# Retention in groups of 128 tokens, one of them shared by two batches, and one transfer queue issued in step with the outputs

## The chip, the cores and the metric

The kernel runs on one core of one Trainium2 chip. The core has a matrix engine (PE, with its weight loads PEld), a vector engine (DVE), an activation engine (ACT), a general engine (POOL) and a sequencer that only starts transfers (SP). Transfers can be started from SP (called SPq in the trace), ACT (ACTq) and POOL (POOLq). The metric is the device time of one execution in microseconds (us), the median of several runs.

## The reference

```
scores = (1/sqrt(64)) * q @ k^T             # 8 batches, 8 heads, 576 tokens, 64 wide
ret    = scores * gamma_h^(i-j)  for i >= j, else 0
x      = ret @ v                            # heads side by side: 4608 tokens x 512
h      = x @ w_in                           # 512 -> 2048
out    = (h * cos(h)) @ w_out               # 2048 -> 512, float32
```

## The kernel before

Retention is computed in chunks: each batch of 576 tokens is cut into four chunks of 128 and one of 64, so there are 40 chunks. `load` brings q, k and v of a chunk (float32, in pieces of 64 numbers) by three transfers from SP. `prep` scales q and k by powers of gamma (POOL, for the first four chunks k on DVE), casts v, and from chunk 8 on starts two DMA transposes on SP that turn scaled q and k into `qkT`; the first eight chunks are transposed on PE (`tr`). On PE a chunk is then: `scores` (tile `sc`, masked on DVE into `ret`), `state` (tile `st`, the running sum of k^T v of the batch, masked into `sb`), and `attn_out` (tile `ov`, from `sb` and from `ret`, copied on DVE into `xT`).

The two dense products run over ten tiles of tokens, `widths` = 512, 256, 256, then seven of 512; they are called tile 0 to 9 here. For a tile, `mm1` makes 16 blocks `h` (four matmuls each), ACT takes the cosine, DVE multiplies into `gT`; `mm2` then adds up 16 matmuls for each 128 tokens into `o`, ACT copies `o` to `ot`, and a transfer writes it out (output 0 to 35, one for each 128 tokens). The retention pieces of the next tile are laid between the `mm2` matmuls, after each four of them.

The order on each engine is the order of the code. `feed`, called from `scores`, issues loads and preps ahead: chunk c+4 is prepared and chunk c+10 loaded when chunk c has its scores. Outputs are started from ACT, loads and transposes from SP, weights from POOL (`w_in` in four parts, `w_out` in four parts). Three early loads wait for weight parts (`GATED`). Each transfer from SP or ACT takes the next of eight completion counters in the order in which the code issues it, and waits for the transfer that held this counter before it, whichever of the two queues that one stands in. PSUM has four buffers for `h` and `o`; `ot` has four buffers.

Of the kernel before, what the change touches and what calls it, by code (L numbers as in the profile page):

```python
# [17 lines left out]
def kernel(  # L18
# [13 lines left out]

    nc = tc.nc
# [8 lines left out]
    NC = (S + P - 1) // P  # L42
    csz = [min(P, S - c * P) for c in range(NC)]
# [8 lines left out]
    chunks = [(b, c) for b in range(B) for c in range(NC)]  # L52
# [22 lines left out]
    pos_i = consts.tile([P, NC, H], I32)  # L75
    pos = consts.tile([P, NC, H], F32)
    lng = consts.tile([P, H], F32)
    gq = consts.tile([P, NC, H], F32)
    gk = consts.tile([P, NC, H], F32)
    ln_scale = consts.tile([P, 1], F32)  # L80
    half_pi = consts.tile([P, 1], F32)
    tri = consts.tile([P, P], F32)
    diag2 = consts.tile([P, P], F32)
# [7 lines left out]
    def load(g):  # L91

        b, c = chunks[g]
        sz = csz[c]
        first = None
        for name, src in (("q", q), ("k", k), ("v", v)):
            f = ld.tile([P, H, D], F32, tag="f" + name, name=f"f{name}")
            i = nc.sync.dma_start(  # L98
                f[:sz], src[b, :, c * P : c * P + sz, :].rearrange("h s d -> s h d")
            )  # L100
            first = first or i
            tiles["f" + name, g] = f
        return first

    def prep(g, eng_k, eng_v):

        b, c = chunks[g]
        sz = csz[c]
# [3 lines left out]
        tq = gq[:sz, c, :].unsqueeze(2).to_broadcast([sz, H, D])  # L112
        tk = gk[:sz, c, :].unsqueeze(2).to_broadcast([sz, H, D])
        nc.gpsimd.tensor_tensor(out=qks[:sz, 0], in0=fq[:sz], in1=tq, op=ALU.mult)  # L114
        eng_k.tensor_tensor(out=qks[:sz, 1], in0=fk[:sz], in1=tk, op=ALU.mult)  # L115
        if eng_v is nc.scalar:
            nc.scalar.copy(vb[:sz], fv[:sz])
        else:
            eng_v.tensor_copy(vb[:sz], fv[:sz])  # L119
        qkT = trp.tile([P, 2, HG, P], BF16, tag="qkT", name="qkT")  # L120
        if g >= N_PE_T:
            for m in range(2):
                nc.sync.dma_start(  # L123
                    qkT[:, m, :, :sz],
                    qks[:sz, m].rearrange("s h d -> s (h d)"),
                    transpose=True,
                )
        tiles["a", g] = (qks, vb, qkT)

    def transposes(g):  # L130
        sz = csz[chunks[g][1]]
        qks, vb, qkT = tiles["a", g]
        ps = ps_ov.tile([P, 2, HG, P], BF16, tag="ov", name="tr")
        for m in range(2):
            for hg in range(HG):
                nc.tensor.transpose(  # L136
                    ps[:, m, hg, :sz],
                    qks[:sz, m, 2 * hg : 2 * hg + 2, :].rearrange("s h d -> s (h d)"),
                    ident[:sz, :sz],
                )  # L140
        nc.vector.tensor_copy(qkT[:, :, :, :sz], ps[:, :, :, :sz])  # L141

    def scores(g):
        if g >= 4:
            feed(g + 1 + LEAD)
        sz = csz[chunks[g][1]]
        qks, vb, qkT = tiles["a", g]
        ps = ps_sc.tile([P, 2, HG, P], F32, tag="sc", name="sc")
        for hg in range(HG):
            for he in range(2):  # L150
                d0 = he * D
                nc.tensor.matmul(  # L152
                    ps[:sz, he, hg, :sz],
                    lhsT=qkT[d0 : d0 + D, 1, hg, :sz],
                    rhs=qkT[d0 : d0 + D, 0, hg, :sz],
# [3 lines left out]
        ret = retp.tile([P, 2, HG, P], BF16, tag="ret", name="ret")  # L159
        nc.vector.tensor_tensor(  # L160
            out=ret[:sz, :, :, :sz].rearrange("p a b i -> p (a b) i"),
# [160 lines left out]
    for u in units(0, 4):  # L322
        u()
# [82 lines left out]
```

## Time and profile before

| | |
|---|---|
| median of 3 runs | 357.11 us (355.91 to 357.18) |
| the profiled execution | 357.89 us, of it 356.2 us span from the first to the last instruction |
| PE busy | 307.8 us (86%) |
| DVE, ACT, POOL busy | 200.1, 128.1, 105.6 us |
| read from HBM, written | 36.70 MB, 9.44 MB |

The span is what the trace shows; 1.7 us of the profiled time lie around it. An engine's share of busy time is a mean over stages that have different limits.

### The profile page before, as it was taken

The page shows a single profiled execution, that of the slowest core. Times are in us where ns is not written, and L with a number is a line of the kernel's source. Part 1 is how long each engine was busy: PE and PEld are TensorE (multiplying, and loading weights), DVE is VectorE, ACT ScalarE, POOL GpSimd, SP SyncE. Part 2 cuts the span into 40 slices and gives each one's busy share as a digit, 9 for nine tenths or more (in the row PEclk, how much of TensorE's full clock was granted, in tenths as well). Part 3 has the DMA queues.
Part 4 walks back from the last instruction along what each step waited for, and adds up shares of the span by engine and source line. Part 5 has one row for each costly group of instructions (what it writes and reads, how often), then busy time and mean ns, then how long its engine had stood idle before and what let it go on. Part 6 is the DMA issues. An engine that isn't in the chain of part 4 may idle for free.

```text
span 356.2 us, 5733 instructions
## 1 busy us (share of the span) xinstructions
PE 307.8 (86%) x2176; PEld 155.3 (44%) x2176; DVE 200.1 (56%) x299; ACT 128.1 (36%) x204; POOL 105.6 (30%) x128
## 2 busy tenths in 40 slices
PE   1078999203999999999999999999999999999995
PEld 0054445101747544454444444444444544454442
DVE  2387745000767858666853776486468648844710
ACT  2123700002708057107513831471175118414721
POOL 3630467705041640571055017502800300000000
PEclk9989999855799999999999999999999999999999
DMA  9999999999967997899679809961610310011011
GB/s 175 211 209 205 192 202 192 208 196 216 228 133 170 222 198 151 187 211 220 123 153 240 154 18 215 217 112 45 142 39 0 83 57 26 1 61 59 2 46 72
DMA packets 153180, 49.80 MB, mean 140 GB/s; under 512 B 144448, under 2 KB 148032, under 8 KB 153152
## 3 DMA queue, kind: packets, MB, share of 16 engines
q1 hardware_dynamic: 143744, 35.80, 56.3%
q10 hardware_dynamic: 5184, 9.44, 7.9%
q0 software_dynamic: 4224, 4.19, 7.1%
q8 instruction: 17, 0.28, 0.3%
q14 instruction: 11, 0.09, 0.1%
HBM read 36.70 MB, written 9.44 MB: 130 GB/s over the span
## 4 chain that ended last, share of the span: by engine, by line
PE 80%; DMA 7%; SPq 5%; DVE 4%; issue 1%; ACT 1%; POOL 1%; ACTq 0%; POOLq 0%
PE o L262 35%; PE h L246 35%; SPq L98 4%; PE ov L211 3%; PE sc L152 3%; DMA fk<-in_k_dram 3%; DMA qkT<-qks 2%; PE ov L201 2%; PE st L175 2%; DMA fv<-in_v_dram 2%; SPq L123 1%; DVE ret L160 1%; PE tr L136 1%; DVE qkT L141 1%; DVE xT L220 1%
## 5 line engine op out<-in xcount | busy, mean ns | idle before, releaser
L246 PE MATMUL h<-xT,w_in_sb 128*128 128x512 bf16 (+1 forms) x640 | 129.7, 364 | 23.4 <-ACT ot L271 21.8
L255 DVE TENSOR_TENSOR gT<-h,cosh 128x512 bf16<-128x512 f32 (+1 forms) x160 | 101.5, 638 | 76.7 <-ACT cosh L254 76.3
L262 PE MATMUL o<-w_out_sb,gT 128*128 128x512 bf16 x576 | 143.0, 380 | 0.7 <-DVE gT L255 0.7
L254 ACT ACTIVATE cosh<-h,half_pi 128x512 f32<-128x512 f32 (+1 forms) x160 | 101.5, 644 | 35.6 <-PE h L246 34.5
L246 PEld LDWEIGHTS <-w_in_sb 128*128 128x128 bf16 x640 | 63.8, 100 | 88.0 <-issue 24.8
L271 ACT COPY ot<-o 128x512 f32<-128x512 f32 x36 | 21.1, 585 | 172.9 <-PE o L262 150.3
L262 PEld LDWEIGHTS <-gT 128*128 128x128 bf16 x576 | 49.5, 98 | 50.7 <-issue 0.5
L119 POOL CAST vb<-fv 128x512 bf16<-128x512 f32 (+1 forms) x36 | 21.9, 608 | 132.4 <-PE ov L211 119.2
L114 POOL TENSOR_TENSOR qks<-fq,gq 128x512 bf16<-128x512 f32 (+1 forms) x40 | 41.6, 1040 | 42.1 <-DMA fq<-in_q_dram 30.0
L160 DVE TENSOR_TENSOR ret<-sc,tri 128x1024 bf16<-128x1024 f32 (+1 forms) x40 | 44.5, 1113 | 16.4 <-PE sc L152 16.4
L115 POOL TENSOR_TENSOR qks<-fk,gk 128x512 bf16<-128x512 f32 (+1 forms) x36 | 37.4, 1040 | 1.3 <-DMA fk<-in_k_dram 1.2
L220 DVE CAST xT<-ov 128x512 bf16<-128x512 f32 (+1 forms) x40 | 25.5, 637 | 17.5 <-PE ov L211 16.5
L184 DVE TENSOR_TENSOR sb<-st,diag_104 128x512 bf16<-128x512 f32 x32 | 22.0, 686 | 12.3 <-PE st L175 12.3
L136 PE MATMUL tr<-ident,qks 128*128 128x128 bf16 (+1 forms) x64 | 6.1, 249 | 17.2 <-DVE qkT L141 10.7
L152 PE MATMUL sc<-qkT 64*128 64x128 bf16 (+1 forms) x320 | 15.8, 221 | 1.6 <-DVE qkT L141 0.8
L211 PE MATMUL ov<-ret,vb 128*64 128x128 bf16 (+1 forms) x320 | 16.2, 224 | 0.6 <-DVE qkT L141 0.6
L152 PEld LDWEIGHTS <-qkT 64*128 64x128 bf16 (+1 forms) x320 | 9.3, 99 | 16.5 <-issue 14.5
L136 PEld LDWEIGHTS <-qks 128*128 128x128 bf16 (+1 forms) x64 | 4.8, 112 | 19.5 <-issue 9.5
L201 PEld LDWEIGHTS <-sb 128*128 128x128 bf16 x128 | 9.5, 100 | 8.3 <-issue 1.3
L211 PEld LDWEIGHTS <-vb 128*64 128x64 bf16 (+1 forms) x320 | 10.1, 111 | 6.5 <-issue 3.7
L175 PE MATMUL st<-vb,qks 128*128 128x128 bf16 x128 | 12.9, 225 | 0.0
L201 PE MATMUL ov<-qkT,sb 128*128 128x128 bf16 (+1 forms) x128 | 11.9, 218 | 1.0 <-DVE xT L220 0.6
(26 smaller groups left out, 32.0 us busy)
## 6 DMA issues: line engine op xcount, KB each, us to landing
out_dram<-ot ACTq DMA_DIRECT2D x36, 256.0 KB, 3.2
fq<-in_q_dram SPq DMA_DIRECT2D x32, 256.0 KB, 4.2
fk<-in_k_dram SPq DMA_DIRECT2D x32, 256.0 KB, 4.8
fv<-in_v_dram SPq DMA_DIRECT2D x32, 256.0 KB, 5.0
w_out_sb<-in_moe_w_out_dram POOLq DMA_DIRECT2D x4, 512.0 KB, 16.1
w_in_sb<-in_moe_w_in_dram POOLq DMA_DIRECT2D x1, 1024.0 KB, 11.4
fq<-in_q_dram SPq DMA_DIRECT2D x8, 128.0 KB, 3.6
fk<-in_k_dram SPq DMA_DIRECT2D x8, 128.0 KB, 3.9
```

What stands on the lines that cost most here:

```text
L114: nc.gpsimd.tensor_tensor(out=qks[:sz, 0], in0=fq[:sz], in1=tq, op=ALU.mult)
L115: eng_k.tensor_tensor(out=qks[:sz, 1], in0=fk[:sz], in1=tk, op=ALU.mult)
L152: nc.tensor.matmul(ps[:sz, he, hg, :sz], lhsT=qkT[d0 : d0 + D, 1, hg, :sz], rhs=qkT[d0 : d0 + D, 0, hg, :sz], start=True, stop=True,)
L160: nc.vector.tensor_tensor(out=ret[:sz, :, :, :sz].rearrange("p a b i -> p (a b) i"), in0=ps[:sz, :, :, :sz].rearrange("p a b i -> p (a b) i"),
L184: nc.vector.tensor_tensor(out=sb, in0=ps, in1=diag2.unsqueeze(1).to_broadcast([P, HG, P]), op=ALU.mult,)
L201: nc.tensor.matmul(ps[:, hg, :sz], lhsT=sb[:, hg, :], rhs=qkT[:, 0, hg, :sz], start=(hg == 0), stop=False, skip_group_check=True,)
L211: nc.tensor.matmul(ps[he * D : he * D + D, hg, :sz], lhsT=vb[:sz, 2 * hg + he, :], rhs=ret[:sz, he, hg, :sz], start=(c == 0 and hg == 0), ...
L220: nc.vector.tensor_copy(xT[:, :, t0 : t0 + sz], ps[:, :, :sz])
L246: nc.tensor.matmul(ps[:, :w], lhsT=w_in_sb[:, dg, et * P : (et + 1) * P], rhs=xT[:, dg, t0 : t0 + w], start=(dg == 0), stop=(dg == DG - 1),)
L254: nc.scalar.activation(cosh[:, :w], ps[:, :w], ACTF.Sin, bias=half_pi, scale=1.0)
L255: nc.vector.tensor_mul(gT[:, et, :w], ps[:, :w], cosh[:, :w])
L262: nc.tensor.matmul(ps, lhsT=gT[:, et, tsi * P : (tsi + 1) * P], rhs=w_out_sb[:, et, :], start=(et == 0), stop=(et == ET - 1),)
```

## The change

Chunks become 36 groups of 128 consecutive tokens. Two batches are nine groups (`PER`); the middle one (`MIX` = 4) holds the last 64 tokens of one batch and the first 64 of the next, is loaded by six transfers of half the size, has a mask of its own (`tri_mix`), and starts a new state from its second half. All transfers from SP stand in one order written in `feed(s)`, which is called once for each output s, just after its transfer, which moves from ACT to SP: up to 11 groups ahead are loaded, up to 9 prepared, and groups up to s+7 are transposed, by one DMA transpose of twice the width in the place of two. The first four groups are now prepared, transposed, scored and summed one after the other, where before all four were prepared first; the copies of `tr` into `qkT` move from DVE to ACT. The first tile's `mm1` runs over two halves of 256 tokens in an order of blocks written by hand (`first`), and in 256-wide tiles two blocks share a PSUM bank, one cosine and one product. In tile 0 the `mm2` matmuls run output by output, and retention of the next tile is put into their second half (`late`). Groups 4 and 5 wait for the second part of `w_out`.

```
-    AHEAD = 6
-    LEAD = 4
-    GATED = {4: 4, 5: 6, 6: 7}
+    NG = NTOK // P
+    PER = 2 * S // P
+    MIX = PER // 2
+    HP = P // 2
     N_PE_T = 8
...
-    ld = ctx.enter_context(tc.tile_pool(name="ld", bufs=7))
-    nat = ctx.enter_context(tc.tile_pool(name="nat", bufs=7))
-    trp = ctx.enter_context(tc.tile_pool(name="trp", bufs=7))
+    ld = ctx.enter_context(tc.tile_pool(name="ld", bufs=6))
+    nat = ctx.enter_context(tc.tile_pool(name="nat", bufs=8))
+    trp = ctx.enter_context(tc.tile_pool(name="trp", bufs=8))
...
+        if g % PER == MIX:
+            parts = [(0, HP, t0), (HP, P, t0 + HP)]
...
     def transposes(g):
         qks, vb, qkT = tiles["a", g]
         if g >= N_PE_T:
+            nc.sync.dma_start(qkT, qks.rearrange("s m h d -> s (m h d)"), transpose=True)
+            return
...
-        nc.vector.tensor_copy(qkT[:, :, :, :sz], ps[:, :, :, :sz])
+        nc.scalar.copy(qkT, ps)
     def scores(g):
-        if g >= 4:
-            feed(g + 1 + LEAD)
...
     def mm2(n, tsi, et):
...
             nc.scalar.copy(ot, ps)
-            t0 = starts[n] + tsi * P
-            nc.scalar.dma_start(out[t0 : t0 + P, :], ot)
+            s = starts[n] // P + tsi
+            nc.sync.dma_start(out[s * P : (s + 1) * P, :], ot)
+            feed(s)
+    def feed(s):
+        nonlocal loaded, prepared, transposed
+        while loaded < min(NG, 2 * s + 8, s + 11):
+            load(loaded)
+            loaded += 1
+        while prepared < min(NG, loaded, 2 * s + 7, s + 9):
+            prep(prepared)
+            prepared += 1
+            if transposed < N_PE_T:
+                transposed += 1
+        while transposed < min(prepared, s + 8):
+            transposes(transposed)
+            transposed += 1
...
     for g in range(4):
-        prep(g, nc.vector, nc.scalar)
-        if g == 2:
+        if g == 0:
+            prep(g, early=True)
+        if g == 3:
             load_w_in(0, 256)
             load_w_in(256, 512)
+            load_w_in(512, 1024)
+            load_w_in(1024, 2048)
+            w_dma = [load_w_out(e, e + 4) for e in range(0, ET, 4)]
+            load(4, gate=w_dma[1])
+            load(5)
...
+        transposes(g)
+        nc.scalar.copy(tiles["a", g][1], tiles.pop(("fv", g)))
+        scores(g)
+        state(g)
+        if g < 3:
+            prep(g + 1, early=True)
+            attn_out(g)
+    for g in (4, 5):
+        prep(g)
+    first = [(0, 0), (0, 4), (1, 0), (0, 8), (1, 4), (0, 12), (1, 8), (1, 12)]
+    for i, (half, et) in enumerate(first):
+        mm1(0, et, half * 256, 256)
+        if i == 0:
+            attn_out(3)
+        mm1(0, et + 2, half * 256, 256)
     for n, w in enumerate(widths):
...
-        if n == 0:
-            mms = [(tsi, et) for et in range(ET) for tsi in range(nts)]
-        else:
-            mms = [(tsi, et) for tsi in range(nts) for et in range(ET)]
+        mms = [(tsi, et) for tsi in range(nts) for et in range(ET)]
...
-            want = -(-total * (i + 1) // max(1, len(groups) - 2))
+            late = len(groups) // 2 if n == 0 else 0
+            want = -(-total * (i + 1 - late) // max(1, len(groups) - 2 - late))
             while todo and total - len(todo) < want:
                 todo.pop(0)()
```

First place, SP's queue when the first outputs are made. Before, from the last load of chunk 13 over the load of chunk 14 to the first DMA transposes (chunks 8 and 9); no output stands in this queue.

```order
L98 DMA fv_423<-in_v_dram 128x8x64
L98 DMA fq_596<-in_q_dram 64x8x64
L98 DMA fk_598<-in_k_dram 64x8x64
L98 DMA fv_600<-in_v_dram 64x8x64
L123 DMA_TRANSPOSE qkT_607<-qks_602 128x4x128 x2
L98 DMA fq_643<-in_q_dram 128x8x64
L98 DMA fk_645<-in_k_dram 128x8x64
L98 DMA fv_647<-in_v_dram 128x8x64
L123 DMA_TRANSPOSE qkT_654<-qks_649 128x4x64 x2
```

Now, from output 1 (ot_627) over the loads of groups 8 and 9 to the transpose of group 8 and output 2 (ot_710).

```order
L283 DMA out_0_dram<-ot_627 128x512
L102 DMA fq_630<-in_q_dram 128x8x64
L102 DMA fk_632<-in_k_dram 128x8x64
L102 DMA fv_634<-in_v_dram 128x8x64
L102 DMA fq_636<-in_q_dram 128x8x64
L102 DMA fk_638<-in_k_dram 128x8x64
L102 DMA fv_640<-in_v_dram 128x8x64
L137 DMA_TRANSPOSE qkT_650<-qks_648 128x8x128
L283 DMA out_0_dram<-ot_710 128x512
```

The outputs have moved into this queue, and a load stands behind the output that calls for it; before, all 15 first loads stood ahead of the first transpose. From here the queue goes on as output 2, loads 10 and 11, transpose 9, output 3, loads 12 and 13, transpose 10, output 4, load 14, transpose 11.

Second place, SP's queue now in the first of the 512-wide tiles behind the small ones (tile 3, outputs 8 to 11): the transpose of group 14, output 8 (ot_1522), the load of group 18, the transpose of group 15 (qkT_1343), output 9 (ot_1587).

```order
L137 DMA_TRANSPOSE qkT_1259<-qks_1257 128x8x128
L283 DMA out_0_dram<-ot_1522 128x512
L102 DMA fq_1525<-in_q_dram 128x8x64
L102 DMA fk_1527<-in_k_dram 128x8x64
L102 DMA fv_1529<-in_v_dram 128x8x64
L137 DMA_TRANSPOSE qkT_1343<-qks_1341 128x8x128
L283 DMA out_0_dram<-ot_1587 128x512
```

The transpose of group s+7 now stands behind output s and behind the load of group s+10; this pattern repeats for each output up to 25. Before, transposes and loads alternated in the same way, with the output in another queue.

Third place, ACT while tile 0 ends. Before, with the outputs' transfers between the copies:

```order
L254 ACTIVATE cosh<-h,half_pi 128x512 x16
L271 COPY ot<-o 128x512
L273 DMA out_dram<-ot 128x512
L271 COPY ot<-o 128x512
L273 DMA out_dram<-ot 128x512
```

Now:

```order
L264 ACTIVATE cosh<-h,half_pi 128x512 x16
L281 COPY ot<-o 128x512 x2
L147 COPY qkT<-tr 128x1024 x2
L281 COPY ot<-o 128x512 x2
L264 ACTIVATE cosh<-h,half_pi 128x512 x8
```

No transfer stands in ACT's order any more; two copies of transposed groups stand between the outputs' copies.

## Rows read from the trace of the kernel before

**Rows 1.** The page: forty equal slices of the span (8.9 us each).

```profile
PEclk9989999855799999999999999999999999999999
GB/s 175 211 209 205 192 202 192 208 196 216 228 133 170 222 198 151 187 211 220 123 153 240 154 18 215 217 112 45 142 39 0 83 57 26 1 61 59 2 46 72
```

**Rows 2.** PE by time: start, length, line, tile, idle before and what ended it.

```profile
63.91 0.60 PE L246 MATMUL h<-xT,w_in_sb 128*128 128x256 bf16 x4
82.73 1.01 PE L246 MATMUL h<-xT,w_in_sb 128*128 128x256 bf16 x4 [18.22 <-ACT ot L271]
...
96.53 1.03 PE L262 MATMUL o<-w_out_sb,gT 128*128 128x512 bf16 x4
...
107.40 1.91 PE L246 MATMUL h<-xT,w_in_sb 128*128 128x256 bf16 x16
109.64 5.40 PE L246 MATMUL h<-xT,w_in_sb 128*128 128x256 bf16 x48 [0.33 <-DVE gT L255]
114.88 1.03 PE L262 MATMUL o<-w_out_sb,gT 128*128 128x512 bf16 x4
...
127.01 13.98 PE L246 MATMUL h<-xT,w_in_sb 128*128 128x512 bf16 x64
```

**Rows 3.** ACT and its transfer at the end of the gap.

```profile
81.67 0.38 ACTq L273 DMA_DIRECT2D out_dram<-ot  x1
82.09 0.58 ACT L271 COPY ot<-o 128x512 f32<-128x512 f32 x1 [18.23 <-DMA qkT<-qks]
```

**Rows 4.** Early loads on SP that waited for weight parts (start, length).

```profile
30.89 0.72 SPq L98 DMA_DIRECT2D fq<-in_q_dram  x1
...
36.23 0.39 SPq L98 DMA_DIRECT2D fq<-in_q_dram  x1
```

**Rows 5.** POOL: the third part of w_in, then the page's landing time of the fourth.

```profile
16.09 1.55 POOL L303 DMA_DIRECT2D w_in_sb<-in_moe_w_in_dram  x2
...
w_in_sb<-in_moe_w_in_dram POOLq DMA_DIRECT2D x1, 1024.0 KB, 11.4
```

**Rows 6.** The page's group of POOL scaling q (count, busy us, mean ns, idle before).

```profile
L114 POOL TENSOR_TENSOR qks<-fq,gq 128x512 bf16<-128x512 f32 (+1 forms) x40 | 41.6, 1040 | 42.1 <-DMA fq<-in_q_dram 30.0
```

**Rows 7.** PE in mm2 of a later tile: pieces of retention between the o matmuls.

```profile
175.33 0.40 PE L152 MATMUL sc<-qkT 64*128 64x128 bf16 x8
175.66 1.04 PE L262 MATMUL o<-w_out_sb,gT 128*128 128x512 bf16 x4
176.53 0.39 PE L175 MATMUL st<-vb,qks 128*128 128x128 bf16 x4
176.76 1.03 PE L262 MATMUL o<-w_out_sb,gT 128*128 128x512 bf16 x4
...
178.83 0.39 PE L201 MATMUL ov<-qkT,sb 128*128 128x128 bf16 x4
...
179.49 1.90 PE L262 MATMUL o<-w_out_sb,gT 128*128 128x512 bf16 x8
```

**Rows 8.** SP's queue in a later, quiet stretch (start, length).

```profile
211.59 2.47 SPq L123 DMA_TRANSPOSE qkT<-qks  x2
214.11 0.57 SPq L98 DMA_DIRECT2D fq<-in_q_dram  x1
...
216.14 2.95 SPq L123 DMA_TRANSPOSE qkT<-qks  x2
```

**Rows 9.** DMA issues of 211.5 to 212.8, 216.1 to 217.4, 221.6 to 222.9: us to landing.

```profile
qkT<-qks SPq DMA_TRANSPOSE x1, 3.7
...
qkT<-qks SPq DMA_TRANSPOSE x1, 5.5
...
qkT<-qks SPq DMA_TRANSPOSE x1, 6.8
```

**Rows 10.** Windows of tile 3 and tile 9: length, busy us of each engine, clock, DMA.

```profile
127.10:160.60 33.50, 33.50 (x242) 16.04 (x241) 22.38 (x30) 13.32 (x20) 14.04 (x17) 1.00 1.00 191
...
324.60:356.20 31.60, 27.70 (x129) 12.36 (x127) 11.04 (x16) 13.90 (x21) 0.00 (x0) 0.99 0.11 42
```

More of the change, by code (lines that the diff above doesn't have):

```diff
@@ L111, in prep, with transposes @@
         vb = nat.tile([P, H, D], BF16, tag="vb", name="vb")
[L112 to L117, printed above, removed]
-        else:
-            eng_v.tensor_copy(vb[:sz], fv[:sz])
-        qkT = trp.tile([P, 2, HG, P], BF16, tag="qkT", name="qkT")
-        if g >= N_PE_T:
[L122 to L133, printed above, removed]
+        qkT = trp.tile([P, 2 * HG, P], BF16, tag="qkT", name="qkT")
+        tq = gq[:, c, :].unsqueeze(2).to_broadcast([P, H, D])
+        tk = gk[:, c, :].unsqueeze(2).to_broadcast([P, H, D])
+        nc.gpsimd.tensor_tensor(out=qks[:, 0], in0=fq, in1=tq, op=ALU.mult)
+        (nc.vector if early else nc.gpsimd).tensor_tensor(
+            out=qks[:, 1], in0=fk, in1=tk, op=ALU.mult
+        )
+        tiles["a", g] = (qks, vb, qkT)
+        tiles["fv", g] = fv
+        if not early:
+            nc.gpsimd.tensor_copy(vb, tiles.pop(("fv", g)))
+    def transposes(g):
+        qks, vb, qkT = tiles["a", g]
+        if g >= N_PE_T:
+            nc.sync.dma_start(qkT, qks.rearrange("s m h d -> s (m h d)"), transpose=True)
+            return
+        ps = ps_ov.tile([P, 2 * HG, P], BF16, tag="ov", name="tr")
         for m in range(2):
@@ L168, in state @@
     def state(g):
-        b, c = chunks[g]
+        c = g % PER
+        if c == PER - 1:
+            return
         qks, vb, qkT = tiles["a", g]
-        if c == 0:
-            tiles["stps", b] = ps_st.tile([P, HG, P], F32, tag="st", name="st")
-        ps = tiles["stps", b]
+        first = c in (0, MIX)
+        if first:
+            tiles["stps"] = ps_st.tile([P, HG, P], F32, tag="st", name="st")
+        ps = tiles["stps"]
+        p0 = HP if c == MIX else 0
         for hg in range(HG):
@@ L320 @@
-    for g0 in range(0, ET, 4):
-        load_w_out(g0, g0 + 4)
-    for u in units(0, 4):
-        u()
-    def gate(ins, w):
-        tc.add_manual_dep(
-            ins.ins, w.ins.name,
-            mybir.DependencyInfo(mybir.DependencyClass.Sync, mybir.DependencyReason.DATA),
-            reason="weights first",
-        )
-    loaded, prepared = 4, 4
-    def feed(n):
-        nonlocal loaded, prepared
-        while loaded < len(chunks) and (loaded < n + AHEAD or prepared < n):
-            i = load(loaded)
-            if loaded in GATED:
-                gate(i, w_dma[GATED[loaded]])
-            loaded += 1
-            if prepared < n and prepared + AHEAD < loaded:
-                prep(prepared, nc.gpsimd, nc.gpsimd)
-                prepared += 1
-        while prepared < min(n, len(chunks)):
-            prep(prepared, nc.gpsimd, nc.gpsimd)
-            prepared += 1
@@ L353 @@
+    for g in (4, 5):
+        prep(g)
+    loaded = prepared = transposed = 6
+    first = [(0, 0), (0, 4), (1, 0), (0, 8), (1, 4), (0, 12), (1, 8), (1, 12)]
[4 more added lines that the diff above has]
+        mm1(0, et + 2, half * 256, 256)
     for n, w in enumerate(widths):
-        for et in range(ET):
-            mm1(n, et)
-        need = done
+        if n > 0:
+            for et in range(0, ET, 512 // w):
+                mm1(n, et, 0, w)
+        todo = []
@@ L357 @@
         if n + 1 < len(widths):
[L358 to L361 removed]
+            g0 = starts[n + 1] // P
+            todo = units(g0, g0 + widths[n + 1] // P)
         total = len(todo)
[L363 removed]
         nts = w // P
[L365 to L368 removed]
+        mms = [(tsi, et) for tsi in range(nts) for et in range(ET)]
```

164 lines of the change are left out of this document (84 added, 80 removed).

## The prediction

> **What bounds the kernel now.** I read the page's slices first, then PE by time, then who made PE wait. In the slices TensorE's granted clock shows one hole, in slices 10 to 12 (80 to 107 us); transfers move 192 to 228 GB/s through the same stretch [rows 1]. PE by time says why: it starts the first 256-wide mm1 at 63.91, does one block, and stands for 18.22 us; three more blocks come at 82.73 and later, and only from 96.53 is it in mm2 of tile 1 [rows 2]. What ended the wait is ACT's copy of an output, since an output's copy frees the PSUM buffer that the next h block needs. ACT was not busy: its second copy at 82.09 had waited 18.23 us, behind its own output transfer, which could be issued only at 81.67, when a transpose from SP had landed [rows 3]. That is the counter rule: the output took a counter whose last holder is a transfer that SP's queue reached only then. So before 127 us the kernel is bound by an order between two queues. From 127.10 PE is busy in every microsecond at full clock (33.50 of 33.50 in tile 3), until 324.60; tile 9 and the last output take 31.6 [rows 10]. I cost the change in three stretches: up to mm1 of tile 3 (127.0 now [rows 2]), tiles 3 to 8 (127.1 to 324.6, 197.5), tile 9 (31.6).
>
> **Stretch 1: up to mm1 of tile 3.** Outputs, loads and transposes now stand in one queue in the order in which counters are given, so no counter can be held by a later row, and ACT waits for PE alone. Two limits are left, and I take the later one at each point.
>
> Transfers. The slices from 8.9 to 62.3 us have a mean of 202 GB/s (211, 209, 205, 192, 202, 192) [rows 1]; I take that for all kinds. The gate of groups 4 and 5 is the second part of w_out; before, the first part opened a load at 30.89 and the third at 36.23 [rows 4], so the second falls at about 33.5. It can't be much later now: the weights are issued some 3 us later, but nothing else competes. Behind the gate come two parts of w_out (1.05 MB as bf16) and groups 4 and 5 (0.786 MB each): 2.62 MB, 13.0 us, 46.5. Then, by the order of the queue, up to the transpose of group 11: nine loads (7.08 MB), four transposes (1.05 MB), five outputs (1.31 MB): 9.44 MB, 46.7 us, 93.2. I add 1 us for SP's stand at the first transpose (it waits until POOL has scaled group 8, with output 2 and loads 10 and 11 behind it): 94.
>
> PE. The fourth part of w_in is issued about 16.9 and lands 11.4 later, 28.3 [rows 5]. Three pairs of first-tile blocks run before it; the other five pairs are 80 matmuls of 256 columns at 0.1125 (5.40 for 48 [rows 2]): 37.3. Eight groups of four o matmuls and one more, at 0.87 [rows 7], give 45.2; there PE transposes groups 4 and 5, and group 5 needs two scalings of 1.04 [rows 6] behind its landing: about 47.5. So the earlier start of mm1 (groups one by one) and the two-block cosines are hidden behind that wait; without this cover they would be worth the 2 us between 45.2 and 47.5 and no more. From 47.5: two groups of transposes 0.9, seven groups of o 6.1, and retention of two groups 2.5 (sc 0.33, st 0.23, ov 0.66 each [rows 7]): 57. Tile 1 as before but without its stall: mm1 64 x 0.1125 = 7.2, mm2 with two groups 10.9 (96.53 to 107.40): 75. Tile 2: mm1 7.5 (107.40 to 114.88), mm2 with four full groups about 12 (12.1 before): 94.5 with no wait. But the scores of group 11 stand behind four of its eight o groups, at about 89, and their transpose lands at 94. From there: 0.33 + 4 x 0.87 + two ov 1.32 + st 0.23 = 5.4, so tile 3 starts at about 99. **Gain 28.** Bounds: 94.5 with no wait for transfers (32), and 105 if SP's stands cost as much again at each of the four transposes as POOL's three operations do (22).
>
> The Trainium skill, "DMA: Bandwidth & Descriptors", section Latency and other measured facts, has DMA transposes at an effective 261 GB/s where the middle dimension is not contiguous. By that a group's 262 kB would take an estimated 1.0 us against 1.3 at the slices' rate, and four of them here with five more below would bring the sum from 338 to about 335. No row here isolates one, so I stay with the slices.
>
> **Stretch 2: tiles 3 to 8.** PE's work hardly changes: a tile has now 128 big matmuls (27.6), four sc, four ov, three or four st, and 0.09 for the o group ahead of each sc: about 32.7, six of them 196.5, against 197.5. **Gain 1.** POOL, ACT and DVE each stay far below PE there (14.04, 13.32 and 22.38 of 33.50 [rows 10]); fewer, fuller ret and xT operations, the moved copies and the wider cosines cost or give nothing, with PE as their cover.
>
> What is new is the place of the transposes. The last group of the next tile is group s+7 for the first output s of a tile. Its transpose stands in SP's queue behind output s and behind three loads, and PE comes to its scores in the same mm2. From the end of output s on PE to these scores there are, by the rule for `want`, six o groups (5 x 0.87 + 0.96), two ov, two st and one sc: 7.4 us in tiles 3, 5 and 7; where one of the four groups has no state (tiles 4 and 6), five o groups, two ov, one sc, one st: 6.3. SP needs: copy 0.58 and issue 0.38 [rows 3], three loads up to the transpose 2.03 (214.11 to 216.14), so the transpose starts at 3.0. Behind three loads a pair of transposes lands 5.5 after its start, behind none 3.7 [rows 8, 9]. The changed kernel's single transpose of double width doesn't occur in this trace; its bytes and place are those of the pair, so I take 5.5, with 0.4 for the output's data ahead: 8.9. Waits: 1.5 three times, 2.6 twice, 9.7 us. **Loss 10.** Bounds: at 3.7 it lands at 6.7, waits 0.8 in all; at 6.8, the longest of the rows, it lands at 10.2, 16.2 in all. In tile 8 no loads are left, so it lands at 4.7 and nobody waits.
>
> **Stretch 3** keeps its work; the last output is issued from SP instead of ACT at a like cost.
>
> **Sum**, against the profiled execution: 356.2 - 28 - 1 + 10 = 337.2 of span; with the 1.7 around it 338.9, against 357.9. The median of the runs before lies 0.8 under the profiled one, so 338.
>
> **Rivals.**
> (a) The transposes come in time: the wide one is faster than the pair or overtakes the loads. Then stretch 2 has no new wait, 338 - 9 = 329. For: a pair with nothing ahead lands in 3.7. Against: 5.5 and 6.8 behind loads. 0.22.
> (b) Transfers are short for longer: SP stands at each transpose of groups 8 to 11 until POOL is done, and DMA runs dry; tile 3 starts at 105 or later, 344 to 349. For: one queue, everything behind the waiting row. Against: a load stands ahead of the first transpose, and the groups of the later ones are long loaded. 0.15.
> (c) Slower: the last transpose of a tile is late by far more. Its place is the same, five waits of 3.4 + x less 7.4 or 6.3, together 5x - 18, where x is its time to landing; this eats the 29 us gained from x = 9.4 on. Nothing in the rows is over 6.8. Where a transpose of double width took twice the 5.5, x = 11, the kernel would be at 365. 0.05.
> (d) No change: the hole at 64 to 97 was a shortage of data as much as of PSUM (the slices there still move 196 to 228 GB/s), and the time comes back as waits for loads. Against: by its own rate the new order needs 18 MB up to group 11, and 202 GB/s carry them by 94. 0.03.
>
> **How the numbers follow.** My forecast has 0.55, at 338 (its own range 333 to 343). Between 326 and 349 lie it, (a) and nearly all of (b). Faster by over 0.5% (about what a measurement here can tell from no change) is the forecast, (a) and (b): 0.92; (d) 0.03; (c) 0.05.
>
> **What would show it.** In the changed kernel's profile: no copy of ot that waits for a transpose; the granted clock full from about 45 us on; mm1 of tile 3 starting near 99, preceded by a wait of the sc matmuls of group 11 for DMA; in tiles 3 to 7 one idle stretch of PE each, 1 to 3 us, ended by the DMA transpose, and none in tile 8; tile 9 unchanged. The prediction is wrong if tile 3 starts after 110 or before 93, or if the waits in tiles 3 to 7 are nil or above 4 us each.

## The result: 337.5 us, and the profile after

The changed kernel takes 337.51 us (median of 4 runs, 336.54 to 338.0). The kernel before took 357.12 us beside it (4 runs, 355.91 to 357.18). The ratio is 0.9455, with a 95% interval of 0.9425 to 0.9485. The profiled execution took 338.0 us, 335.8 of it span. In the prediction's three stretches:

| | before | predicted | measured |
|---|---|---|---|
| up to mm1 of tile 3 | 127.0 | 99 | 100.9 |
| tiles 3 to 8 (from there to mm1 of tile 9) | 197.5 | 206.2 | 203.6 |
| of these, waits for transposed tiles | 0 | 9.7 | 6.3 |
| tile 9 and the last output | 31.6 | 31.6 | 31.3 |

The page's slices are 8.4 us each now. The lines are PE's busy tenths, the granted clock and the transfer rate.

```profile
PE   2559998989899998999699999998999899999995
...
PEclk9999999999999999999999999999999999999999
...
GB/s 174 201 140 202 211 194 243 209 200 223 187 253 213 20 136 233 249 10 102 207 261 59 90 210 266 61 103 223 237 66 94 205 141 3 62 66 31 0 60 67
```

The hole of [rows 1] is gone: no slice of the clock is under 9, and from the fourth slice to the last but one PE is below 8 tenths only once (6, from 159.5 to 167.9 us, in tile 4). The next view lists who waited for whom (us in all, times, longest).

```profile
PE sc L155 <- DMA qkT<-qks: 6.3, 4, 2.6
...
PE sc L155 <- ACT qkT L147: 4.4, 4, 1.1
ACT ot L281 <- DMA fq<-in_q_dram: 3.8, 1, 3.8
```

The 18 us stand of [rows 2, 3] has no counterpart. The view puts one output copy's 3.8 us down to a load, but PE's last matmuls for that output end at 135.17 and the copy starts at 135.21: it waited for PE, like the last copies of the other tiles. PE's waits fall into two sets: small ones for ACT and DVE, and four for DMA transposes. PE by time shows where both lie; first the stretch up to tile 3.

```profile
11.47 1.01 PE L142 MATMUL tr<-ident,qks 128*128 128x128 bf16 x8 [1.16 <-DVE xT L227]
13.59 0.60 PE L155 MATMUL sc<-qkT 64*128 64x128 bf16 x8 [1.10 <-ACT qkT L147]
...
17.44 1.01 PE L142 MATMUL tr<-ident,qks 128*128 128x128 bf16 x8 [1.29 <-DVE xT L227]
...
23.29 1.01 PE L142 MATMUL tr<-ident,qks 128*128 128x128 bf16 x8 [1.16 <-DVE xT L227]
...
26.35 1.91 PE L256 MATMUL h<-xT,w_in_sb 128*128 128x256 bf16 x8
...
29.19 14.31 PE L256 MATMUL h<-xT,w_in_sb 128*128 128x256 bf16 x120
43.34 7.93 PE L272 MATMUL o<-w_out_sb,gT 128*128 128x512 bf16 x35
51.11 0.61 PE L142 MATMUL tr<-ident,qks 128*128 128x128 bf16 x8
52.82 0.61 PE L142 MATMUL tr<-ident,qks 128*128 128x128 bf16 x8 [1.10 <-ACT qkT L147]
```

An early group takes PE 5.9 to 6.0 us (11.47 to 17.44 to 23.29). Inside, PE waits for ACT's copy of the transposed tile, and at the end for DVE's `xT`. The first h block starts at 26.35, and 120 of the 128 matmuls of tile 0's mm1 run only from 29.19 on. POOL's side of the same stretch is the scaling of group 5:

```profile
48.24 1.04 POOL L126 TENSOR_TENSOR qks<-fk,gk 128x512 bf16<-128x512 f32 x1
```

It ends at 49.28, before PE is ready for groups 4 and 5 (51.11 and 52.82). PE next, from the scores of group 11 on:

```profile
95.50 0.40 PE L155 MATMUL sc<-qkT 64*128 64x128 bf16 x8
...
100.86 13.98 PE L256 MATMUL h<-xT,w_in_sb 128*128 128x512 bf16 x63
...
127.92 0.40 PE L155 MATMUL sc<-qkT 64*128 64x128 bf16 x8 [1.02 <-DMA qkT<-qks]
...
162.43 0.40 PE L155 MATMUL sc<-qkT 64*128 64x128 bf16 x8 [2.57 <-DMA qkT<-qks]
...
229.42 0.40 PE L155 MATMUL sc<-qkT 64*128 64x128 bf16 x8 [1.28 <-DMA qkT<-qks]
...
264.54 0.40 PE L155 MATMUL sc<-qkT 64*128 64x128 bf16 x8 [1.46 <-DMA qkT<-qks]
...
304.47 13.98 PE L256 MATMUL h<-xT,w_in_sb 128*128 128x512 bf16 x63
```

The scores of group 11 wait for nothing, so no transfer stands in the way of tile 3. Their transpose is issued on SP at 87.52 and lands 6.0 us later, at 93.5, 2 us before PE comes to them:

```profile
87.52 3.83 SPq L137 DMA_TRANSPOSE qkT<-qks  x1
```

Later, tiles 3, 4, 6 and 7 have one wait each and tiles 5 and 8 have none. SP's queue shows what these waits are made of (start, length), in tile 3 and then in tile 4:

```profile
120.03 0.36 SPq L283 DMA_DIRECT2D out_dram<-ot  x1
120.45 0.43 SPq L102 DMA_DIRECT2D fq<-in_q_dram  x1
120.93 0.70 SPq L102 DMA_DIRECT2D fk<-in_k_dram  x1
121.67 0.89 SPq L102 DMA_DIRECT2D fv<-in_v_dram  x1
122.67 3.29 SPq L137 DMA_TRANSPOSE qkT<-qks  x1
...
154.18 0.36 SPq L283 DMA_DIRECT2D out_dram<-ot  x1
154.59 1.36 SPq L102 DMA_DIRECT2D fq<-in_q_dram  x2
...
158.78 1.29 SPq L137 DMA_TRANSPOSE qkT<-qks  x1
```

Three loads stand between output and transpose, six of half the size where the group is the shared one. The DMA view gives the landing of these two transposes, 5.2 and 3.6 us after their start:

```profile
qkT<-qks SPq DMA_TRANSPOSE x1, 5.2
...
qkT<-qks SPq DMA_TRANSPOSE x1, 3.6
```

122.67 + 5.2 is 127.9 and 158.78 + 3.6 is 162.4: PE's scores start as the data land.

### The profile page after: what moved, and what is told of

Its sections match the earlier page's. It is cut to its first block, busy times and chain, and to the rows that moved or that the text cites. A ratio compares the mean times of both kernels' runs of the same rounds, so it can differ in the third digit from the quotient of the medians.

```text
span 335.8 us, 5512 instructions
## 1 busy us (share of the span) xinstructions
PE 303.4 (90%) x2142; PEld 162.2 (48%) x2176; DVE 191.8 (57%) x267; ACT 133.2 (40%) x196; POOL 97.8 (29%) x120
## 4 chain that ended last, share of the span: by engine, by line
PE 81%; DMA 9%; ACT 3%; DVE 3%; issue 2%; SPq 1%; DVEq 0%; POOLq 0%; POOL 0%
PE h L256 38%; PE o L272 32%; DMA qkT<-qks 6%; PE sc L155 4%; PE ov L219 3%; DMA fq<-in_q_dram 2%; ACT qkT L147 2%; PE st L183 2%; PE tr L142 2%; PE ov L209 1%; DMA fk<-in_k_dram 1%; DVE ret L164 1%; SPq L102 1%; ACT ot L281 1%; DVE qks L126 1%
## 5 line engine op out<-in xcount | busy, mean ns | idle before, releaser
L265 DVE TENSOR_TENSOR gT<-h,cosh 128x512 bf16<-128x512 f32 x144 | 99.6, 692 | 55.6 <-ACT cosh L264 55.6
L264 ACT ACTIVATE cosh<-h,half_pi 128x512 f32<-128x512 f32 x144 | 98.9, 687 | 29.7 <-PE h L256 29.7
L125 POOL TENSOR_TENSOR qks<-fq,gq 128x512 bf16<-128x512 f32 x36 | 37.5, 1042 | 153.5 <-DMA fq<-in_q_dram 145.7
L164 DVE TENSOR_TENSOR ret<-sc,tri 128x1024 bf16<-128x1024 f32 x32 | 39.1, 1222 | 30.2 <-PE sc L155 30.2
L126 POOL TENSOR_TENSOR qks<-fk,gk 128x512 bf16<-128x512 f32 x32 | 33.3, 1042 | 6.7 <-DMA fk<-in_k_dram 5.4
L227 DVE CAST xT<-ov 128x512 bf16<-128x512 f32 x36 | 24.8, 689 | 16.1 <-PE ov L219 16.1
L155 PE MATMUL sc<-qkT 64*128 64x128 bf16 x288 | 15.1, 228 | 12.2 <-DMA qkT<-qks 6.3
L132 POOL CAST vb<-fv 128x512 bf16<-128x512 f32 x32 | 19.5, 609 | 10.5 <-DMA fv<-in_v_dram 6.9
L219 PE MATMUL ov<-ret,vb 128*64 128x128 bf16 x288 | 15.8, 234 | 1.6 <-DVE ret L164 1.6
L147 ACT COPY qkT<-tr 128x1024 bf16<-128x1024 bf16 x8 | 8.1, 1012 | 19.8 <-PE tr L142 19.8
L183 PE MATMUL st<-vb,qks 128*128 128x128 bf16 (+1 forms) x128 | 13.3, 230 | 0.0
## 6 DMA issues: line engine op xcount, KB each, us to landing
w_out_sb<-in_moe_w_out_dram POOLq DMA_DIRECT2D x4, 512.0 KB, 17.4
w_in_sb<-in_moe_w_in_dram POOLq DMA_DIRECT2D x1, 1024.0 KB, 12.1
```

Of the source, the lines that this page charges most:

```text
L125: nc.gpsimd.tensor_tensor(out=qks[:, 0], in0=fq, in1=tq, op=ALU.mult)
L126: (nc.vector if early else nc.gpsimd).tensor_tensor(out=qks[:, 1], in0=fk, in1=tk, op=ALU.mult)
L155: nc.tensor.matmul(ps[:, he, hg, :], lhsT=qkT[d0 : d0 + D, HG + hg, :], rhs=qkT[d0 : d0 + D, hg, :], start=True, stop=True,)
L164: nc.vector.tensor_tensor(out=ret.rearrange("p a b i -> p (a b) i"), in0=ps.rearrange("p a b i -> p (a b) i"), in1=mask.unsqueeze(1).to_br ...
L183: nc.tensor.matmul(ps[:, hg, :], lhsT=qks[p0:, 1, 2 * hg : 2 * hg + 2, :].rearrange("s h d -> s (h d)"), rhs=vb[p0:, 2 * hg : 2 * hg + 2, ...
L219: nc.tensor.matmul(ps[he * D : he * D + D, hg, :], lhsT=vb[:, 2 * hg + he, :], rhs=ret[:, he, hg, :], start=(c == 0 and hg == 0), stop=(hg ...
```

## The experiments

Eleven kernels were run. Nine are edits of the changed kernel, two of the kernel before. "This" is the changed kernel at 337.5 us, whose mm1 of tile 3 starts at 100.86.

### Transposes ahead of loads

```
     def feed(s):
+        while N_PE_T <= transposed < min(prepared, s + 8):
+            transposes(transposed)
+            transposed += 1
         while loaded < min(NG, 2 * s + 8, s + 11):
```

> The changed kernel, but feed(s) issues the transpose of group s+7 ahead of the loads instead of behind them. Theory A (the waits of 1.0, 2.6, 1.3 and 1.5 us before sc in tiles 3, 4, 6 and 7, 6.3 us in all, come from the transpose's place behind three or six loads): the waits go, 337.5 - 6 = 331.5 us. Rival B (the wide transpose itself is slow, or DMA has too much to carry): the transpose starts 2 us earlier but lands no more than 1 us earlier, at least 4 us of the waits stay, 335 us or more.

Measured: 331.13 us (330.62 to 331.5), ratio 0.9252 (0.9224 to 0.928). SP in tile 3 of this kernel:

```profile
120.24 0.36 SPq L283 DMA_DIRECT2D out_dram<-ot  x1
120.70 1.29 SPq L137 DMA_TRANSPOSE qkT<-qks  x1
122.05 0.57 SPq L102 DMA_DIRECT2D fq<-in_q_dram  x1
```

The transpose starts 0.46 after the output in place of 2.64, and no scores wait for a transfer any more. Tile 3 starts at 101.06, 0.2 later than in the changed kernel, so the whole 6.4 us come from tiles 3 to 8. The place of the transpose behind the loads is the cause of the new waits. Without them the six tiles take 298.02 - 101.06 = 196.96, or 32.8 each.

### Two transposes of half the width

```
-            nc.sync.dma_start(qkT, qks.rearrange("s m h d -> s (m h d)"), transpose=True)
+            for m in range(2):
+                nc.sync.dma_start(
+                    qkT[:, m * HG : (m + 1) * HG, :],
+                    qks[:, m].rearrange("s h d -> s (h d)"),
+                    transpose=True,
+                )
```

> The changed kernel (337.5 us) with each DMA transpose of double width put back into two of half width, at the same place in the queue. The prediction's step says that the wide one stands for its pair, in bytes and place: then the waits of the scores for transposed tiles in tiles 3 to 7 stay at 5 to 8 us in all (6.3 in the changed kernel) and the time at 337 to 340 us. Rival: the width itself makes it late or early: then these waits change by more than 3 us in one direction, and the time by as much, below 335 or above 340 us.

Measured: 339.65 us (338.49 to 340.76), ratio 0.9499 (0.9448 to 0.955). Waits of the scores, in all, times, longest:

```profile
PE sc L160 <- DMA qkT<-qks: 7.0, 4, 2.8
```

7.0 for 6.3, where other kernels here with the wide transpose have 6.3 to 7.2: the runs show no difference by the width, and the prediction's step (the wide one stands for its pair) holds. The intervals of the two kernels' ratios overlap. What the profiled execution is longer by lies mostly in a lower granted clock, told under the hardware below.

### Outputs from ACT again

```
-            nc.sync.dma_start(out[s * P : (s + 1) * P, :], ot)
+            nc.scalar.dma_start(out[s * P : (s + 1) * P, :], ot)
```

> The changed kernel with one part undone: outputs are issued from ACT again, with the code order of loads, transposes and outputs as it is. Theory A (the hole at 64 to 97 us went because loads and transposes are now issued in the code in step with outputs, so that a counter's last holder is never far behind; which queue the outputs stand in matters little): no wait of 18 us, 336 to 339 us. Rival B (the one queue did it): ACT waits again for transfers that SP has not reached, 345 us or more.

Measured: 338.47 us (338.01 to 339.31), ratio 0.9461 (0.943 to 0.9491). That is the changed kernel's time, but made up differently. ACT by time:

```profile
62.96 0.59 ACT L281 COPY ot<-o 128x512 f32<-128x512 f32 x1 [5.58 <-DMA fq<-in_q_dram]
68.77 0.34 ACTq L283 DMA_DIRECT2D out_dram<-ot  x1
69.21 1.27 ACT L264 ACTIVATE cosh<-h,half_pi 128x512 f32<-128x512 f32 x2 [5.67 <-DMA fk<-in_k_dram]
```

PE behind it:

```profile
70.68 5.97 PE L256 MATMUL h<-xT,w_in_sb 128*128 128x256 bf16 x32 [5.08 <-DVE gT L265]
```

ACT stands twice at its own transfers, for counters that loads on SP hold: by the trace, the output at 62.58 takes the counter of a load that landed at 62.50, the one at 68.77 that of a load that landed at 68.69. PE then idles 5.08 at 70.68, and its next 32 matmuls take 5.97 in place of the 3.66 of the 32 before, at a granted clock of 0.50 (1.00 before). Tile 3 starts at 108.28, 7.4 later. But the scores of tiles 3 to 7 never wait for a transpose, since SP's loads and transposes no longer stand behind an output that waits for its data: 6.3 back. Moving the outputs cost about what it gave, in two different stretches, beside the other edits. The time is in theory A's range, but not for its reason: the queue of the outputs matters, once in each direction.

### The kernel before, its outputs from another engine

```
-            nc.scalar.dma_start(out[t0 : t0 + P, :], ot)
+            nc.gpsimd.dma_start(out[t0 : t0 + P, :], ot)
```

> The kernel before, with one edit: outputs are issued from POOL, whose transfers take other counters than those of SP and ACT; loads and transposes stand as they were. Theory A (the hole at 64 to 82 us is the wait of an output for a counter whose holder SP has not reached): PE's stand of 18.2 us goes or shrinks below 6 us, 336 to 345 us. Rival B (there was no data for PE in that stretch, prediction's rival d): the stand stays as a wait for loads or transposes, 350 us or more.

Measured: 342.5 us (one run). PE goes from the first blocks of tile 1 at 63.83 to the rest at 66.12 without a stand, and tile 3 starts at 109.57 in place of 127.01:

```profile
66.12 5.40 PE L246 MATMUL h<-xT,w_in_sb 128*128 128x256 bf16 x48 [0.23 <-DVE gT L255]
```

Two waits for transposes appear, 2.22 at 78.30 and 2.73 at 102.65.

The same line with `nc.sync`, the order of the code left as it was:

> The kernel before, with one edit: outputs are issued from SP, in the code order of before, so all transfers stand in one queue but the loads and transposes are not in step with the outputs. Theory A (the order of the issues makes the hole, not the number of queues): the first output stands behind the same loads and transposes, ACT's second, third or fifth copy waits for it, and PE stands as long as before, 352 us or more. Rival B (one in-order queue is what removes the hole): 345 us or less.

Measured: 341.85 us (one run), so theory A fell. ACT, SP and PE by time in this kernel:

```profile
65.42 2.05 ACT L271 COPY ot<-o 128x512 f32<-128x512 f32 x4 [18.08 <-PE o L262]
...
86.93 2.00 SPq L273 DMA_DIRECT2D out_dram<-ot  x4
...
89.31 1.28 ACT L271 COPY ot<-o 128x512 f32<-128x512 f32 x2 [15.05 <-DMA out_dram<-ot]
...
89.95 9.08 PE L246 MATMUL h<-xT,w_in_sb 128*128 128x256 bf16 x56 [4.45 <-ACT ot L271]
```

The outputs leave as late as before (86.93 here, 81.67 in [rows 3]). But ACT is free: it copies four outputs at once at 65.42, PE goes on, and only the fifth copy waits, since `ot` has four buffers. PE loses 4.45 us there and tile 3 starts at 111.00. So the 18 us were never the late output. They were ACT, which works in order, standing at its own issue with the copies that free PSUM behind it.

### The pairs of blocks in tiles 1 and 2 taken out

```
-        m = 512 // w
+        m = 512 // w if n == 0 else 1
...
-            for et in range(0, ET, 512 // w):
+            for et in range(ET):
```

> The changed kernel, but in tiles 1 and 2 each h block has a PSUM buffer, a cosine and a product of its own again (tile 0 keeps its pairs). Prediction's step: hidden behind PE, 337.5 us give or take 1. Rival: ACT at 0.47 us and DVE at 0.42 us for 256 columns fall behind PE's 0.45 us a block, and tiles 1 and 2 take 1 to 2 us longer each, 339 to 341 us.

Measured: 339.86 us (339.01 to 340.15), ratio 0.9493 (0.9463 to 0.9523). The time lies in the rival's range, but its reason fails. From the start of tile 1 to that of tile 3 this kernel takes 38.7 us (61.64 to 100.31) and the changed kernel 38.8 (62.08 to 100.86), so the pairs give nothing in the stretch in which they act. What the profiled execution is longer by comes later, from a wait that is 3.40 in place of 2.57 in tile 4 and from the granted clock behind it. The intervals of the two kernels' ratios overlap.

### The order of the early groups

First, each group's transposes ahead of the `attn_out` of the group before:

```
-        transposes(g)
+        if g == 0:
+            transposes(g)
...
         if g < 3:
             prep(g + 1, early=True)
+            transposes(g + 1)
             attn_out(g)
```

> The changed kernel, but PE transposes early group g+1 ahead of attn_out of group g. Theory A (stretch 1 is set by PE's chain through the first four groups, 6.0 us a group, since from the first h block at 26.35 us PE hardly stands until tile 3): the first h block comes at about 21 us and tile 3 3 to 5 us earlier, 333 to 335 us. Rival B (as the prediction had it, stretch 1 is set by transfers: group 5 is scaled at 49.3, group 11's transpose lands at 93.5): the first block comes earlier, PE then waits for group 5, and tile 3 starts at most 2 us earlier, 335.5 us or more.

Measured: 338.83 us (337.63 to 340.83), ratio 0.9457 (0.942 to 0.9493); the first h block at 26.43, not earlier. PE stands at the second half of each transpose for DVE's scaling of k (1.49, 1.83, 1.61), which now stands behind `ret` and `sb` on DVE: the chain moved to another engine. Inconclusive on what the early chain is worth.

Then the order of the kernel before, all four groups prepared first (the weights are still issued behind the fourth group's loads):

```
     for g in range(4):
-        if g == 0:
-            prep(g, early=True)
+        prep(g, early=True)
...
+    transposes(0)
+    for g in range(4):
+        if g < 3:
+            transposes(g + 1)
         nc.scalar.copy(tiles["a", g][1], tiles.pop(("fv", g)))
         scores(g)
+        if g > 0:
+            attn_out(g - 1)
         state(g)
-        if g < 3:
-            prep(g + 1, early=True)
-            attn_out(g)
```

> The changed kernel, but the first four groups are prepared first (all four scalings by POOL ahead), and then transposed and scored in the overlapped order of the kernel before; the outputs, the pairs and the one queue stay. Theory A, TensorE's own early chain sets the first stretch: the first h block starts later than 26.35 us (about 30), h of tile 3 starts 2 to 5 us later than 100.86, and the time is 340 to 342 us. Rival B, an early start is hidden behind the transfers that scale group 5 at 49.3 us: h of tile 3 starts at most 1 us later, and the time is 337 to 339 us.

Measured: 337.94 us (335.05 to 338.34), ratio 0.9436 (0.9384 to 0.9489). The first h block is at 26.43 and tile 3 at 99.70, 1.2 earlier than in the changed kernel; 1.0 of this is that 120 matmuls of tile 0 take 13.27 in place of 14.31, which goes with TensorE's clock (told under the hardware below). Theory A fell on the order: one group after the other brings nothing over all four first. PE by time shows the stand that takes the place of the small ones:

```profile
18.13 0.61 PE L155 MATMUL sc<-qkT 64*128 64x128 bf16 x8 [4.14 <-DVE ret L164]
```

DVE has the scalings of k of the later groups ahead of `ret`. This fits rival B's time, but not its reason, as the next kernel shows.

### Both moves at once, on top of the first experiment

```
-        transposes(g)
+        if g == 0:
+            transposes(g)
+        if g < 3:
+            prep(g + 1, early=True)
...
         if g < 3:
-            prep(g + 1, early=True)
+            transposes(g + 1)
             attn_out(g)
```

> Run e1_transpose_first with the early groups overlapped in earnest: k of group g+1 is scaled on DVE ahead of the mask of group g, and PE transposes group g+1 ahead of attn_out of group g. Theory A (stretch 1 has two limits close together: PE's early chain and, 2 us below it, the transfers of weights and groups 4 and 5): the first h block comes 3 to 6 us earlier, but PE then waits for POOL's scaling of group 5 (ready at about 49.3 us), and tile 3 starts at most 2 us earlier, 329 to 331 us. Rival B (PE's chain alone): tile 3 starts 3 to 5 us earlier, 325 to 328 us.

Measured: 327.44 us (327.32 to 327.57), ratio 0.9152 (0.9136 to 0.9167). PE by time:

```profile
21.48 1.92 PE L256 MATMUL h<-xT,w_in_sb 128*128 128x256 bf16 x8
...
24.32 4.92 PE L256 MATMUL h<-xT,w_in_sb 128*128 128x256 bf16 x40
30.59 8.91 PE L256 MATMUL h<-xT,w_in_sb 128*128 128x256 bf16 x80 [1.35 <-DMA w_in_sb<-in_moe_w_in_dram]
39.34 7.93 PE L272 MATMUL o<-w_out_sb,gT 128*128 128x512 bf16 x35
```

With `prep` ahead of the scores and the transposes ahead of `attn_out`, the first h block starts 4.9 earlier than in the changed kernel, mm2 of tile 0 4.0 earlier and tile 3, at 96.86, 4.0 earlier (4.2 before the first experiment's). Rival B holds: PE's chain was the limit. The next limit is now close by: POOL has scaled group 5 by 48.70, and PE transposes it at 48.82.

### One piece a step, and weights earlier

The third kernel of this line also rounds `want` down in the first tiles, so that pieces of retention follow each other at some distance:

```
-            want = -(-total * (i + 1 - late) // max(1, len(groups) - 2 - late))
+            if n < 3:
+                want = total * (i + 1 - late) // max(1, len(groups) - 1 - late)
+            else:
+                want = -(-total * (i + 1) // (len(groups) - 2))
```

> Run e7_first_and_overlap, and in tiles 0 to 2 no two pieces of retention are put behind the same four matmuls at the start (rounding down in place of up), so that PE doesn't stand 1.1, 1.1 and 1.4 us for the copy of a transpose and for a mask. Theory A: these three waits go and group 5's transpose is asked for later, 2 to 4 us less than e7. Rival: the last pieces now end later, mm1 of the next tile waits for xT, and nothing is gained.

Measured: 325.59 us (324.88 to 325.65), ratio 0.9094 (0.9079 to 0.9109). Tile 3 starts at 94.44. The three waits of PE for ACT's copies and DVE's `ret` in tiles 0 to 2 (1.10, 1.10 and 1.44 both in the changed kernel and in the run before this one) became 0.24, 0.24 and 0.47. The kernel is 1.85 us faster than the one before, just under theory A's 2 to 4. PE now waits 2.07 for `w_in` at 25.46:

```profile
25.46 13.98 PE L256 MATMUL h<-xT,w_in_sb 128*128 128x256 bf16 x112 [2.07 <-DMA w_in_sb<-in_moe_w_in_dram]
```

The last kernel issues two parts of `w_in` earlier, with `prep(2)` ahead of them:

```
+        if g == 1:
+            prep(2, early=True)
+            load_w_in(0, 256)
+            load_w_in(256, 512)
         if g == 3:
-            load_w_in(0, 256)
-            load_w_in(256, 512)
...
-        if g < 3:
+        if g in (0, 2):
             prep(g + 1, early=True)
```

> The kernel of the run before it with the best time (325.6 us: transposes first, early steps overlapped, one piece a step), but the first two parts of w_in are issued after q of group 2 and not of group 3. There TensorE waited 2.07 us for w_in at 25.46 us. Theory A, this wait lies on the path to h of tile 3: the wait goes, h of tile 3 starts 1 to 2 us earlier than 94.44, and the time is 323.5 to 324.7 us. Rival B, the loads of group 3 land later by as much and TensorE waits for its scaling instead: h of tile 3 at 94 to 95.5, and 325 to 326.5 us.

Measured: 322.94 us (322.44 to 323.31), ratio 0.9033 (0.8998 to 0.9069), the fastest of all. PE by time:

```profile
20.63 1.04 PE L256 MATMUL h<-xT,w_in_sb 128*128 128x256 bf16 x8
...
28.21 8.91 PE L256 MATMUL h<-xT,w_in_sb 128*128 128x256 bf16 x80 [1.03 <-DMA w_in_sb<-in_moe_w_in_dram]
...
44.73 0.61 PE L142 MATMUL tr<-ident,qks 128*128 128x128 bf16 x8
...
92.11 13.98 PE L256 MATMUL h<-xT,w_in_sb 128*128 128x512 bf16 x63
```

Theory A was right in kind and too small: the wait is halved and not gone (2.07 to 1.03), tile 3 starts 2.3 earlier and not 1 to 2, and the time is 0.6 below its range. What the wait doesn't give, the clock does: behind the longer wait of the kernel before, the granted clock was 0.51 from 25.40 to 28.80 and 112 matmuls took 13.98 us, where 0.1125 each (5.40 for 48 in [rows 2]) make 12.6; here 80 took 8.91, and 0.1125 each make 9.0. Group 5 is scaled by 45.7, 3 us earlier, so the queue of weights brought groups 4 and 5 earlier too. From tile 3 to the end this kernel and the one before it take the same 228.3 us (320.4 - 92.11, 322.7 - 94.44), so all of the difference is in the first stretch.

## Why the prediction was right, and where its working was not

**The sign, the size and the first reason** held. The sum was 337.2 us of span and came out at 335.8. What bound the kernel before was read rightly: an order between two queues and ACT behind it. The trace has the counter of each transfer: the output at 81.67 takes the one that the transpose issued at 77.45 held until it landed at 81.60. (Two details are off, and nothing in the sum rests on them. The hole of the granted clock is in slices 8 to 11 of [rows 1], 62 to 98 us, and not in 10 to 12. And the counters aren't given strictly in the code's order: this output's follows that of a load which the code has behind it.) The two runs of the kernel before with outputs elsewhere show it: moving the outputs alone takes 16.0 and 17.4 us of the 26.2 out of the first stretch. All of the change but that move takes 18.7 (127.01 to 108.28), so the two parts overlap and don't add. Which of the other edits makes up the 18.7 stays open: the pairs and the order of the early groups give nothing by themselves, and the rest was not run one by one. The run with outputs on SP also makes the reason narrower than the prediction put it: with the output just as late but issued from SP, the stand of 18 us is a wait of 4.45.

**Stretch 1: the size was right, the limit was the wrong one.** The prediction made transfers the later of the two limits, at 94 for the transpose of group 11, and PE the earlier, at 89 for its scores. The transfers were well sized: the gate of groups 4 and 5 opened at 36.53 (33.5 said), group 5 was scaled by 49.28 (47.5 said), that transpose issued at 87.52 and landed 6.0 later, at 93.5 (94 said). PE was late: its scores of group 11 ran at 95.50, with no wait. The step that failed is "Three pairs of first-tile blocks run before it": 48 matmuls of mm1 were to be done when the fourth part of `w_in` lands at 28.3. Only 8 were, because the chain of the early groups let the first block start no earlier than 26.35. The part itself came later too: it is issued at 18.60 in the changed kernel and lands 12.1 later, at 30.7 (with both moves, where 48 matmuls do run first, the other 80 wait until 30.59). The late start put the end of mm1 at 43.3 in place of 37.3, and PE's transposes of group 4 at 51.1 in place of 45.2, or 3.6 behind the 47.5 to which the prediction had PE stand. Three waits that it priced at nothing, 1.10 and 1.10 for ACT's copies of transposed tiles and 1.44 for `ret`, make PE later again behind that, and the work between took some 0.7 less than its estimate. The last experiment is the proof in reverse. There the fourth part is issued at 16.84, 48 matmuls run first, the other 80 start at 28.21, group 4 is transposed at 44.73, and those are the prediction's 28.3 and 45.2. The two errors nearly cancelled: PE came to the scores of group 11 at 95.50 and not at 89, 6.5 later, and the 5 us of waiting there for their transpose, from 89 to 94, never came. That the stretch came out within 2 us of 99 is luck.

**"Hidden" edits.** The two-block cosines of tiles 1 and 2 are hidden, as said: without them these tiles take 38.7 us and with them 38.8 (tile 0 kept its pairs in that run). The early groups one by one are worth nothing either, but not for the reason given: they don't start mm1 earlier, since all four first gives 26.43 against 26.35. An earlier start itself isn't hidden: 4.9 us earlier moved tile 3 by 4.0. The first block started at 30.50 in the kernel before, and PE's longest early wait there, 10.68 us, was for DVE's copy of `tr`; both orders of the changed kernel have that copy on ACT. That this copy explains the 4 us between 30.50 and 26.35 is argued and was not run.

**Stretch 2: right mechanism, a term mis-sized.** The waits came at the place named, ended by the transfer named, in tiles 3, 4, 6 and 7 and not in tile 8 (tile 5, where one was forecast, had none), and the first experiment removes them by order alone. Their size was put at 1.5 three times and 2.6 twice, 9.7, and was 1.02, 2.57, 0, 1.28 and 1.46, 6.3. The term is the landing of 5.5 from [rows 9], used for all five: measured were 5.2, 3.6, 4.4, 4.3 and 5.5. In tile 4 the landing was short and the wait still 2.57, since the shared group's six loads take SP 4.6 us from the output's start to the transpose (154.18 to 158.78), 2.6 in tile 3; the prediction counted 2.03 for three loads everywhere. PE's own work came to 203.6 - 6.3 = 197.3 us, against 196.5 said and 197.5 before: the gain of 1 is mostly not there.

**Rival (a)** would have needed the waits to vanish; the kernel that removes them by order is at 331.1, near its 329. **Rivals (b), (c) and (d)** are excluded by tile 3 at 100.86, by no wait over 2.57 and by the time.

## What to carry to other kernels

In these kernels an engine that starts a transfer stands at that instruction until the transfer's counter is free, and everything behind it in its program stands too (18.2 us for ACT in the kernel before): give transfers to an engine with nothing urgent behind them, then order its queue by who is waited for first (here transposes before loads, 6.4 us for three moved lines). When two limits come out within a few microseconds of each other, check the chain of small waits that starts the earlier one, since a sum can be right while the limit that it names is the wrong one. One reordering that did nothing by itself, the transposes ahead of `attn_out`, took 4 us off together with a second (which was not run alone), so a null result of one edit doesn't show that the stretch is hidden.

## What the hardware showed that was not expected

**The granted clock after a wait.** After PE's wait of 2.57 us in tile 4 the changed kernel's profile keeps its clock; after 3.40 us at the same place the kernel without pairs does not. Windows of both (length, busy us of PE, PEld, DVE, ACT, POOL, granted clock, DMA share, GB/s), the changed kernel first:

```profile
163.00:166.00 3.00, 3.00 (x24) 1.42 (x23) 1.79 (x2) 0.00 (x0) 0.97 (x1) 1.00 1.17 236
```

```profile
163.00:166.00 3.00, 3.00 (x12) 0.92 (x8) 1.23 (x1) 0.00 (x0) 1.33 (x2) 0.59 1.35 233
```

PE is busy for the whole 3 us in both, but gets through 12 matmuls in place of 24. It was not a matter of length alone: 0.83 in 160 to 170 us with the two half-width transposes (wait of 2.76), 0.78 in 160 to 164 with the first early overlap (wait of 2.46), 0.76 there in 229 to 236 (wait of 1.77). By 203.6 - 6.3 = 197.3 us of work here against 305.93 - 100.03 - 7.0 = 198.9 with the half-width transposes, it cost an estimated 1.6 us in that run. There the waits for transposes cost more than they measure. How much this is in general stays open: another run of the changed kernel had a mean granted clock of 0.995, against 0.999 in the profiled one, at the same span (335.7 and 335.8).

**A half-speed start ahead of the clock's first record.** Eight score matmuls took 0.60 us at 13.59 and 0.40 at 95.50. Eight of 256 columns took 1.91 at 26.35 in the changed kernel and 1.04 at 20.63 in the last experiment, 0.24 and 0.13 each, as at the lower and the higher of TensorE's two levels (1.2 and 2.4 GHz). The windows of 10 to 30 us give a granted clock of 1.00 for both kernels, but this is no reading: the first record of the clock in the trace starts at 31.35 us in the changed kernel and at 18.34 in the last experiment, and time without a record counts as full in a mean. In two kernels whose early phase is that of the changed kernel the first record is at 30.41 (no pairs) and 29.63 (half-width transposes), and the 120 matmuls of tile 0 took 13.83 and 13.47 there, 14.31 in the changed kernel. So differences of up to 1 us in the start of tile 3 between the kernels here can be the clock's and not the edits'. What PE did before differs: in the changed kernel it stood six times for 1.10 to 1.29 us between 11.4 and 25.5, and in the last experiment three times for 1.10 between 10 and 20.6. The doubled matmuls are part of the early chain's price.

**Which queue a transfer stands in.** The Trainium skill, "DMA: Bandwidth & Descriptors", section Rules for kernel authors, says that spreading transfers over SP, ACT and GpSimd doesn't help bandwidth and only saves sequencer issue time. No run here speaks against the first half. The second is too narrow for this kernel: with outputs on ACT the first stretch is 7.4 us longer and the later waits 6.3 us shorter, and neither is issue time; both come from an engine or a queue standing at a transfer in order.

**The copy of a transposed tile.** ACT takes 1012 ns for `qkT<-tr` (128 x 1024, bf16), and PE waits 1.10 us for it in every early group. It is a link of the chain that set the first stretch, and was priced at nothing in the prediction.
